# The scores and weighted sums of a pair of attention units, each spread over two neighbouring steps of the layer beside it

## The chip, the cores and the metric

The kernel runs on one core of a Trainium2 chip. The metric is the device time of one execution in microseconds (us), the median of several runs. The engines are named as in the profile: PE is TensorE's matmul, PEld its weight load, DVE is VectorE, ACT is ScalarE, POOL is GpSimd, SP is SyncE, whose queue (SPq) issues nearly all DMAs here.

## The reference, cut to what matters

Three stages follow one another: an attention with two kinds of masks, a gated layer, and a layer of eight experts with soft assignment to slots.

```
scores = q @ k.T / sqrt(64)          # 4 batches, 8 heads, 576 positions, head size 64
# heads 0-3: a window of 32 positions; heads 4-7: every 4th of 128 positions
attn = softmax(where(mask, scores, -1e9))
x = (attn @ v)                        # -> 2304 tokens x 512
y = (sigmoid(x @ w_gate) * (x @ w_val)) @ w_out        # 512 -> 1536 -> 512
logits = y @ phi                      # 32 slots
...                                   # soft dispatch, 8 experts, soft combination
```

## The kernel before, in words

**Blocks and units.** The 2304 tokens are worked on in five blocks, n = 0 to 4 (512 tokens each, the last 256). The attention of one block is cut into four units, one for each pair of heads (hp); 20 units in all. The masks leave only short windows, so a unit's scores are 32 small matmuls (`score`, L145: 64 rows by 32 columns of weights, 64 columns of data) and its weighted sums are 32 others (`weighted`, L208: 64 by 64; 16 for the plain heads of block 4). Each is shown twice in the profile, since the type is fp32: 64 matmuls and 64 weight loads for one unit's scores.

**The layer.** `l1` computes sigmoid and value of the gated layer for one block and one of 12 slices f of the 1536 columns. For each half a of a slice it runs 12 matmuls of 128x512 (L527) into one of two PSUM banks: for each of four chunks of x, high part of the weights with high and low part of x, then low part of the weights with the high part of x. ACT takes the first half's bank with a sigmoid (L537), DVE the second with a product (L539). Then it calls `between()`. One such group of 12 is a **step** here; blocks 0 and 1 have 24 steps each, counted 1 to 48. For a slice, `split_w` makes the high (ACT, L493) and low part (POOL and DVE, L494) of its weights; in block 0 from `convert` (DMA of the raw form, ACT, DVE, POOL, L421 to L442), in block 1 from a copy in DRAM that `load_w` reads back two slices at a time (L963, tile `wst`).

**The pairs.** Block 0's attention runs before the layer. The 16 units of blocks 1 to 4 run during steps 1 to 48, as eight pairs p = 0 to 7 (`Pairs`). `Pairs.__call__` is part of `between()`: at each step it runs what a table has due. For a pair these are
- `scores` at step SCORES_AT[p]: a mask matmul into each of two banks of `ps_a` (L140; four banks, shared with the turned tiles), 128 score matmuls, `softmax` (DVE max and subtraction, ACT exp, DVE sum and reciprocal, POOL product, L388), and the DMA of the next pair's q and k (L246);
- `turn` of each unit, TURN + TURN_LATE[p] steps later and one more: four transposes (L188) into a bank of `ps_a`, and an ACT copy (L189);
- `sums` at SUMS_AT[p]: the weighted sums into both banks of `ps_m`, the copies out (`finish`), and the DMA of v for the pair after the next (L253).

Block 4's units keep their scores inside the q/k buffer, so the q/k load of pair 7 can only start when the turns of pair 6 are done, unit by unit.

**What sets the order.** The functions are called in the order of the steps, but a scheduler places their instructions on each engine by its own estimate of readiness, within bounds: matmuls and transposes of the pairs (`kept`) stay in the order in which they are written, evictions of the layer's banks come ahead. Each engine, and SP's queue, then executes its list in order. Behind the first pairs two more things are mixed in: from step 25 on small transposes and matmuls of `slot_weights` (L468, L474, L483), and after block 0 the steps of `Post(0)` (L785 logits, L821 transposes, L831, L852, L878), which share the banks of `ps_a` and `ps_m`.

Of the kernel before, what the change touches and what calls it, by code (L numbers as in the profile page):

```python
# [7 lines left out]
F32 = mybir.dt.float32  # L8
# [9 lines left out]
P = 128  # L18
# [12 lines left out]
NRM = True  # L31
C0 = 21
SCORES_AT = (1, 8, 15, 22, 27, 32, 37, 41)
TURN = 4
TURN_LATE = (2, 0, 0, 0, 0, 0, 0, 1)
SUMS_AT = (10, 17, 25, 29, 34, 39, 44, 48)
C1 = 19
WP = 1
ND = 4
# [10 lines left out]
def k_window(n, hp, t, i):  # L50
    if n < 4:
        return 32 * (4 * t + i) if hp < 2 else 160 * i + 32 * t
    return 160 * t + 32 * i if hp < 2 else 64 * (4 * t + i)


def pb_tokens(n):
    return 512 if n < 4 else 256
# [3 lines left out]
def tile_kernel(  # L61
# [17 lines left out]
    ps_a = ctx.enter_context(tc.tile_pool(name="ps_a", bufs=4, space=PSUM))  # L79
    ps_m = ctx.enter_context(tc.tile_pool(name="ps_m", bufs=2, space=PSUM))  # L80
# [11 lines left out]
    mask = msk[:, 0:M_ID].rearrange("p (m c) -> p m c", m=3)  # L92
# [29 lines left out]
    kept = tc.keep_in_program_order  # L122
# [16 lines left out]
    def mask_at(bank, mask_):  # L139
        return nc.tensor.matmul(bank, lhsT=msk[:, M_ID:M_COLS], rhs=mask_, start=True, stop=False, skip_group_check=True)  # L140

    def score(u, t, i, r, to):
        n, hp = u["id"]
        o, d = k_window(n, hp, t, i), slice(64 * r, 64 * r + 64)
        return nc.tensor.matmul(  # L145
            to,
            lhsT=u["qk"][d, 128 * t + 32 * i : 128 * t + 32 * i + 32],
            rhs=u["qk"][d, 512 + o : 512 + o + 64],
            start=False,
            stop=True,  # L150
            skip_group_check=True,
        )

    def scores(u, ts):
        n, hp = u["id"]
        if "s_ps" not in u:
            u["s_ps"] = [ps_a.tile([P, 4, 64], F32, tag="a", name=f"s_ps{r}") for r in range(2)]
            for r in range(2):
                mask_at(u["s_ps"][r].rearrange("p t c -> p (t c)"), mask[:, 1 if hp >= 2 else 0])
        for t in ts:  # L160
            for i in range(4):
                for r in range(2):
                    score(u, t, i, r, u["s_ps"][r][32 * i : 32 * i + 32, t, :])
# [27 lines left out]
    def weighted(u, ts, xp, at=lambda x: x):  # L191

        n, hp = u["id"]
        dil = hp >= 2
        nq = 16 if n == 4 and dil else 32
        p_ = pt_ring[:, u["z"] % 4]
        v = u["v"].rearrange("p (t i r d) -> p t i r d", t=2, i=4, r=2)
        for t in ts:
            for i in range(2 if n == 4 and not dil else 4):
                for r in range(2):  # L200
                    for y in range(2):
                        o, k = xp[y][64 * r : 64 * r + 64, t], slice(64 * y, 64 * y + 64)
                        if dil:
                            o = o.rearrange("p (q f) -> p q f", f=4)[:, :, i]
                        else:
                            o = o[:, 32 * i : 32 * i + 32]
                        at(
                            nc.tensor.matmul(  # L208
                                o, lhsT=v[k, t, i, r, :], rhs=p_[k, 2 * r + t, i, 0:nq], start=True, stop=True
                            )  # L210
                        )
# [26 lines left out]
    def unit_loads(jobs, tags):  # L238
        us = [{"id": j, "z": z} for z, j in enumerate(jobs)]

        def load_qk(z):
            n, hp = jobs[z]
            w = 512 + k_cols(n, hp)
            us[z]["qk"] = b8(tags[z], [P, 2048], F32, "qk")
            us[z]["s"] = sm4[:, z % 4] if n < 4 else us[z]["qk"][:, 1536:2048]
            ld(nc.sync.dma_start(us[z]["qk"][:, 0:w], qkv[n * NHP + hp, :, VCOLS : VCOLS + w]))  # L246

        def load_v(z):
            n, hp = jobs[z]
            if z % 2 == 0:  # L250
                v2 = b8("v", [P, 2, VCOLS], F32, "v2")
                us[z]["v"], us[z + 1]["v"] = v2[:, 0], v2[:, 1]
            ld(nc.sync.dma_start(us[z]["v"], qkv[n * NHP + hp, :, 0:VCOLS]))  # L253

        return us, load_qk, load_v

    def first_attn(weights):
# [3 lines left out]
        def s_step(z, t):  # L261
            if z == 0 and t == 0:
                load_qk(0)
                ld(nc.sync.dma_start(msk, masks.bitcast(BF16)))
                load_qk(1)
                ld(nc.sync.dma_start(cst, consts))
                load_v(0)
                load_qk(2)
                load_v(1)
                weights()  # L270
                load_qk(3)
                load_v(2)
                load_v(3)
            scores(us[z], [t])
            if t == 3:
                softmax(us[z])
# [18 lines left out]
    class Pairs:  # L295


        def __init__(self):
            self.jobs = [(n, hp) for n in range(1, 5) for hp in HP_ORDER]
            self.us, self.qk, self.v = unit_loads(self.jobs, ["qk"] * 16)  # L300
            self.todo = []
            for p in range(8):
                t = SCORES_AT[p]
                late = t + TURN + TURN_LATE[p]
                self.todo += [(t, self.scores, p), (late, self.turn, 2 * p), (late + 1, self.turn, 2 * p + 1)]
                self.todo += [(SUMS_AT[p], self.sums, p)]
            self.todo.sort(key=lambda x: x[0])
            self.n = 0

        def __call__(self):  # L310
            self.n += 1
            while self.todo and self.todo[0][0] <= self.n:
                _, fn, p = self.todo.pop(0)
                fn(p)

        def load(self, what, p):
            if p < 8:
# [3 lines left out]
        def turn(self, z):  # L321
            turn_unit(self.us[z], ps_a, "a", kept)

        def scores(self, p):
            two = self.us[2 * p : 2 * p + 2]
            n = two[0]["id"][0]
            bank = [ps_a.tile([P, 512], F32, tag="a", name=f"s_ps{r}") for r in range(2)]
            for r in range(2):
                m_ = mask[:, 0:2] if n < 4 else mask[:, 2:3].to_broadcast([P, 2, 256])
                kept(mask_at(bank[r].rearrange("p (u c) -> p u c", u=2), m_))  # L330
            for y, u in enumerate(two):
                for t in range(4):
                    for i in range(4):
                        for r in range(2):
                            to = bank[r].rearrange("p (u t c) -> p u t c", u=2, t=4)
                            kept(score(u, t, i, r, to[32 * i : 32 * i + 32, y, t]))
            self.softmax(two, bank)
            self.load(self.qk, p + 1)
            if p == 0:
                self.load(self.v, 1)  # L340

        def sums(self, p):
            two = self.us[2 * p : 2 * p + 2]
            n, hp = two[0]["id"]
            xp = [ps_m.tile([P, 2, 2, pb_tokens(n) // 4], F32, tag="m", name=f"xp{y}") for y in range(2)]
            for y, u in enumerate(two):
                weighted(u, range(2), [x[:, y] for x in xp], kept)
            self.finish(n, hp % 2, xp)
            self.load(self.v, p + 2)

        def softmax(self, two, bank):
# [747 lines left out]
    for f in range(NF):  # L1099
        c = f % 4  # L1100
# [18 lines left out]
    for e in range(8):  # L1119
        for h in range(2):  # L1120
# [8 lines left out]
            tag = reuse.pop(0) if reuse else None  # L1129
# [11 lines left out]
        if e == 2:  # L1141
            rl = sc_[0:1, 192:320].rearrange("o (j s) -> o j s", j=4)
            sums = ps_m.tile([1, P], F32, tag="m", name="sums")
            nc.tensor.transpose(sums, lrun, ident)
            nc.vector.tensor_tensor(rl, re, sums.rearrange("o (j s) -> o j s", j=4), ALU.mult)
            rs = sc_[0:1, 320:352]
            nc.vector.tensor_reduce(rs, rl.rearrange("o j s -> o s j"), AX.X, ALU.add)
            nc.vector.tensor_scalar(rs, rs, 1e-9, None, ALU.add)
            nc.vector.reciprocal(rs, rs)
            nc.vector.tensor_copy(rl, rs.unsqueeze(1).to_broadcast([1, 4, 32]))  # L1150
            rcol = ps_m.tile([P, 1], F32, tag="m", name="rcol")
            nc.tensor.matmul(rcol, lhsT=rl.rearrange("o j s -> o (j s)"), rhs=ident[0:1, 0:1], start=True, stop=True)
            rc = sc_[:, 352:353]
            nc.vector.tensor_copy(rc, rcol)
# [201 lines left out]
```

## Time and profile before

| | |
|---|---|
| median of 3 runs | 499.6 us (498.39 to 499.72) |
| profiled execution, its own time | 498.51 us |
| its span, first to last instruction | 496.7 us |
| mean granted TensorE clock | 0.991 |
| busy, share of the span | PE 94%, PEld 72%, DVE 62%, ACT 49%, POOL 32% |

The span has five parts: a start-up with block 0's attention, steps 1 to 48 (about 35 to 232 us), a stage of blocks 2 and 3 together (to about 357 us), block 4's layer, and the experts. A busy PE includes the overlap of pipelined matmuls, so what counts in the steps is the distance from one group's first matmul to the next group's.

### The profile page before, as it was taken

The numbers are of one execution on the slowest core, as the hardware profiler recorded it, in microseconds if no ns is written. First come the engines' busy times: TensorE is split into PE (matmuls) and PEld (weight loads), VectorE is DVE, ScalarE is ACT, GpSimd is POOL, SyncE is SP. The second block draws the span as 40 slices with busy tenths as digits, with TensorE's granted clock in tenths as the row PEclk, the third lists the DMA queues.
The fourth block names the chain that finished last, engine by engine and source line by source line (L and its number), as shares of the span: only waits on it lengthen the run. The fifth ranks groups of instructions, "written<-read, shape, count | busy, mean of one in ns | idle before, by whom it ended". The sixth has DMA issues, their size and how long they took to land.

```text
span 496.7 us, 12722 instructions
## 1 busy us (share of the span) xinstructions
PE 467.2 (94%) x5470; PEld 356.4 (72%) x5476; DVE 306.4 (62%) x567; ACT 245.1 (49%) x422; POOL 159.7 (32%) x132
## 2 busy tenths in 40 slices
PE   6779999999899999999879999999999999999992
PEld 3558877878677877877448888888887889743552
DVE  3969698976767353554997656656548654531522
ACT  2467566746666453542954554554436544300232
POOL 0243555636283321182244342333312133110100
PEclk9899999999999999999999999999999999999997
DMA  8979899979976401750001220210599785589996
GB/s 325 407 258 345 278 368 313 340 253 376 406 271 212 172 3 49 259 189 3 0 11 76 84 78 9 84 48 38 199 379 422 296 357 215 204 303 379 423 382 217
DMA packets 23784, 112.13 MB, mean 226 GB/s; under 512 B 2352, under 2 KB 7216, under 8 KB 14640
## 3 DMA queue, kind: packets, MB, share of 16 engines
q1 hardware_dynamic: 23408, 111.06, 59.7%
q8 instruction: 43, 0.70, 0.5%
q10 hardware_dynamic: 320, 0.26, 0.2%
q14 instruction: 13, 0.11, 0.1%
HBM read 97.16 MB, written 14.16 MB: 224 GB/s over the span
## 4 chain that ended last, share of the span: by engine, by line
PE 72%; DVE 6%; DMA 4%; ACT 3%; issue 2%; POOL 1%; SPq 0%; DVEq 0%; ACTq 0%
PE l1ps L527 25%; PE pa L651 12%; PE pe L651 6%; PE tp L821 4%; PE h_ps L1122 3%; PE pd L651 3%; PE xp L208 3%; PE so_ps L1181 2%; DMA w<-wg 2%; PE sp L852 2%; PE lt_ps L785 2%; PE s_ps L145 2%; PE wt_ps L468 1%; DVE t_hl L554 1%; PE tr L188 1%
## 5 line engine op out<-in xcount | busy, mean ns | idle before, releaser
L527 PE MATMUL l1ps<-x_hi,whl 128*128 128x512 f32 x384 | 128.9, 402 | 3.2 <-ACT x_hi L229 2.5
L527 PEld LDWEIGHTS l1ps<-x_hi,whl 128*128 128x128 f32 x384 | 72.1, 189 | 20.1 <-ACT x_hi L229 3.2
L527 PE MATMUL l1ps<-x_lo,whl 128*128 128x512 f32 x192 | 76.1, 396 | 0.0
L442 POOL TENSOR_TENSOR fw<-fw 128x512 int32<-128x512 int32 x36 | 51.4, 1437 | 70.8 <-DVE fw L441 35.7
L539 DVE TENSOR_TENSOR g<-l1ps,g 128x512 f32<-128x512 f32 (+1 forms) x36 | 21.6, 600 | 33.6 <-PE l1ps L527 33.2
L527 PEld LDWEIGHTS l1ps<-x_lo,whl 128*128 128x128 f32 x192 | 36.5, 190 | 7.3 <-issue 0.4
L527 PE MATMUL l1ps<-x,whl 128*128 128x256 f32 x288 | 37.3, 286 | 0.1
L527 PEld LDWEIGHTS l1ps<-x,whl 128*128 128x128 f32 x288 | 35.4, 191 | 2.3 <-issue 1.7
L537 ACT ACTIVATE g<-l1ps 128x512 f32<-128x512 f32 (+1 forms) x36 | 18.9, 526 | 32.0 <-PE l1ps L527 31.9
L494 POOL TENSOR_TENSOR whl<-w,whl 128x512 fp32r<-128x512 f32 x12 | 15.9, 1327 | 52.3 <-ACT whl L493 40.7
L821 PE MATMUL tp<-cst,g 128*128 128x128 f32 x216 | 29.1, 275 | 0.1
L494 POOL TENSOR_TENSOR whl<-wst,whl 128x512 fp32r<-128x512 f32 x12 | 16.1, 1342 | 39.1 <-ACT whl L493 33.7
L439 ACT ACTIVATE fw<-st 128x512 f32<-128x512 f32 x36 | 22.7, 674 | 10.0 <-DMA st<-wd 10.0
L821 PEld LDWEIGHTS tp<-cst,g 128*128 128x128 f32 x216 | 24.1, 140 | 4.7 <-ACT g L537 1.7
L494 DVE TENSOR_TENSOR whl<-fw,whl 128x512 fp32r<-128x512 f32 x24 | 23.0, 963 | 6.7 <-ACT whl L493 6.1
L208 PEld LDWEIGHTS xp<-pt_ring,v 64*64 64x64 f32 x1216 | 19.2, 136 | 6.8 <-issue 3.8
L493 ACT CAST whl<-fw 128x512 fp32r<-128x512 f32 x24 | 14.7, 621 | 18.9 <-POOL fw L442 14.6
L826 ACT COPY gt<-tp 128x512 f32<-128x512 f32 x27 | 15.5, 581 | 16.0 <-PE tp L821 12.9
L441 DVE TENSOR_SCALAR fw<-st 128x512 int32<-128x512 uint32 x36 | 21.9, 635 | 2.4 <-DMA st<-wd 2.4
L720 DVE TENSOR_TENSOR tm<-pe,tm 128x512 f32<-128x512 f32 x12 | 8.3, 691 | 23.7 <-PE pe L651 23.7
L208 PE MATMUL xp<-pt_ring,v 64*64 64x32 f32 (+1 forms) x1216 | 20.7, 220 | 2.1 <-ACT pt_ring L189 1.6
L440 DVE TENSOR_SCALAR fw<-fw 128x512 uint32<-128x512 uint32 x36 | 21.0, 592 | 2.1 <-ACT fw L439 1.8
(464 smaller groups left out, 963.9 us busy)
## 6 DMA issues: line engine op xcount, KB each, us to landing
ew<-w SPq DMA_DIRECT2D x32, 1024.0 KB, 8.2
st<-wd SPq DMA_DIRECT2D x18, 1024.0 KB, 9.0
wst<-wg SPq DMA_DIRECT2D x12, 1024.0 KB, 6.8
v<-qkv SPq DMA_DIRECT2D x20, 512.0 KB, 6.5
wg<-fw SPq DMA_DIRECT2D x12, 512.0 KB, 8.0
w<-wg SPq DMA_DIRECT2D x6, 1024.0 KB, 7.6
qk<-qkv SPq DMA_DIRECT2D x10, 576.0 KB, 6.4
qk<-qkv SPq DMA_DIRECT2D x8, 528.0 KB, 5.8
```

Of the source, the lines that this page charges most:

```text
L208: nc.tensor.matmul(o, lhsT=v[k, t, i, r, :], rhs=p_[k, 2 * r + t, i, 0:nq], start=True, stop=True)
L439: nc.scalar.activation(top, st[:, c, 1].bitcast(F32), AF.Prelu, scale=2.0**-112, alpha=2.0**32)
L440: nc.vector.tensor_scalar(top.bitcast(U32), top.bitcast(U32), 3, None, ALU.logical_shift_left)
L441: nc.vector.tensor_scalar(low.bitcast(I32), st[:, c, 0], 2.0**-29, None, ALU.mult)
L442: nc.gpsimd.tensor_tensor(low.bitcast(I32), top.bitcast(I32), low.bitcast(I32), ALU.add)
L494: (nc.gpsimd if pool[h] else nc.vector).tensor_tensor(whl[:, 1, h], src[:, h], whl[:, 0, h].bitcast(F32), ALU.subtract)
L527: nc.tensor.matmul(pt[:, 0:nt], lhsT=whl[:, w_, a, dc, :], rhs=x_[n][:, dc, :], start=first, stop=(dc == HP_ORDER[-1] and w_ == 1),)
L537: nc.scalar.activation(g, pt[:, 0:nt], AF.Sigmoid)
L539: nc.vector.tensor_tensor(g, pt[:, 0:nt], g, ALU.mult)
L651: nc.tensor.matmul(pt, lhsT=w[:, w_, P * c : P * c + P], rhs=x_[:, c], start=first and c == 0 and w_ == 0 and x_ is hi, stop=c == 1 and w_ ...
L821: nc.tensor.transpose(tp[:, c], g_sb[self.n, 4 * q + c][:, P * j : P * j + P], ident)
L826: nc.scalar.copy(to, tp)
```

## The change

`scores` and `sums` are now called once for each unit of a pair, in two neighbouring steps (argument y). The first call takes the banks (and, for scores, writes the masks), the second ends with what followed before: softmax and the next q/k load, or the copies out and the next v load. The banks are kept between the calls in `self.at`. In the table, TURN goes from 4 to 5, counted from the first score step, with other TURN_LATE, so that pairs 1 to 6 turn one step later, and pairs 0 and 7 at the steps where they did. The first call for the sums of pairs 3 to 6 is one step later than the sums were, that of pair 7 one step earlier; pairs 0 to 2 start where they did.

```diff
-TURN = 4
-TURN_LATE = (2, 0, 0, 0, 0, 0, 0, 1)
-SUMS_AT = (10, 17, 25, 29, 34, 39, 44, 48)
+TURN = 5
+TURN_LATE = (1, 0, 0, 0, 0, 0, 0, 0)
+SUMS_AT = (10, 17, 25, 30, 35, 40, 45, 47)
...
-                self.todo += [(t, self.scores, p), (late, self.turn, 2 * p), (late + 1, self.turn, 2 * p + 1)]
-                self.todo += [(SUMS_AT[p], self.sums, p)]
+                self.todo += [(t + y, self.scores, p, y) for y in range(2)]
+                self.todo += [(late + y, self.turn, 2 * p + y) for y in range(2)]
+                self.todo += [(SUMS_AT[p] + y, self.sums, p, y) for y in range(2)]
...
-        def scores(self, p):
+        def scores(self, p, y):
             two = self.us[2 * p : 2 * p + 2]
             n = two[0]["id"][0]
...
+            if y == 0:
+                bank = self.at["s", p] = [ps_a.tile([P, 512], F32, tag="a", name=f"s_ps{r}") for r in range(2)]
+                for r in range(2):
+                    m_ = mask[:, 0:2] if n < 4 else mask[:, 2:3].to_broadcast([P, 2, 256])
+                    kept(mask_at(bank[r].rearrange("p (u c) -> p u c", u=2), m_))
+            bank = self.at["s", p]
+            for t in range(4):
+                for i in range(4):
+                    for r in range(2):
+                        to = bank[r].rearrange("p (u t c) -> p u t c", u=2, t=4)
+                        kept(score(two[y], t, i, r, to[32 * i : 32 * i + 32, y, t]))
+            if y == 0:
+                return
+            self.softmax(two, self.at.pop(("s", p)))
             self.load(self.qk, p + 1)
...
-        def sums(self, p):
+        def sums(self, p, y):
...
-            xp = [ps_m.tile([P, 2, 2, pb_tokens(n) // 4], F32, tag="m", name=f"xp{y}") for y in range(2)]
-            for y, u in enumerate(two):
-                weighted(u, range(2), [x[:, y] for x in xp], kept)
-            self.finish(n, hp % 2, xp)
+            if y == 0:
+                shape = [P, 2, 2, pb_tokens(n) // 4]
+                self.at["x", p] = [ps_m.tile(shape, F32, tag="m", name=f"xp{z}") for z in range(2)]
+            weighted(two[y], range(2), [x[:, y] for x in self.at["x", p]], kept)
+            if y == 0:
+                return
+            self.finish(n, hp % 2, self.at.pop(("x", p)))
             self.load(self.v, p + 2)
```

Two places on PE and one on SP's queue show what moves. The lines of the changed file are 8 higher from `finish` on (L527 is L535 there, L474 L482, L821 L829, L963 L971); a number behind a name tells tiles apart, and "..." stands for further matmuls of the same kind.

**PE, pair 4** (steps 27 and 28; qk_1603 and qk_1605 are its two units before, qk_1636 and qk_1638 after). Before, all scores stand in one run:

```order
L140 MATMUL s_ps1_1829<-msk_75 128x512
L145 MATMUL s_ps0_1828<-qk_1603 32x64
...
L145 MATMUL s_ps0_1828<-qk_1605 32x64
...
L474 MATMUL pt_ps_1912<-pm_91,cst_76 32x256 x4
L468 MATMUL wt_ps_1919<-cst_76,fw_1656 128x128 x4
L527 MATMUL l1ps_1925<-x_hi_1071,whl_1801 128x512
```

After:

```order
L140 MATMUL s_ps1_1823<-msk_75 128x512
L145 MATMUL s_ps0_1822<-qk_1636 32x64
...
L482 MATMUL pt_ps_1858<-pm_91,cst_76 32x256 x4
L476 MATMUL wt_ps_1865<-cst_76,fw_1656 128x128 x4
L535 MATMUL l1ps_1871<-x_hi_1102,whl_1795 128x512
...
L188 MATMUL tr_1885<-cst_76,sm4_172 128x128 x4
L145 MATMUL s_ps0_1822<-qk_1638 32x64
```

Between the two units now stand two kinds of small matmuls, 12 matmuls of the layer and a turn.

**PE, from the turn of pair 6's second unit to the layer's slice f = 10 of block 1** (qk_2242 and qk_2282 hold that unit; whl_3030 and whl_2975 are the split weights of slice 10, whl_2918 and whl_2912 those of slice 9). Before:

```order
L188 MATMUL tr_2900<-cst_76,qk_2242 128x128 x4
L821 MATMUL tp_2906<-cst_76,g_612 128x128 x4
L527 MATMUL l1ps_2923<-x_hi_1071,whl_2918 128x512
...
L145 MATMUL s_ps0_2727<-qk_2568 32x64
...
L527 MATMUL l1ps_2948<-x_hi_1071,whl_2918 128x512
...
L208 MATMUL xp0_2962<-pt_ring_90,v2_2380 64x32
...
L821 MATMUL tp_3024<-cst_76,g_976 128x128 x4
L527 MATMUL l1ps_3035<-x_hi_1071,whl_3030 128x512
```

After:

```order
L188 MATMUL tr_2931<-cst_76,qk_2282 128x128 x4
L829 MATMUL tp_2937<-cst_76,g_612 128x128 x4
L839 MATMUL dt_ps_2943<-cst_76,d_2810 128x128
L535 MATMUL l1ps_2948<-x_hi_1102,whl_2912 128x512
...
L829 MATMUL tp_2969<-cst_76,g_928 128x128 x4
L145 MATMUL s_ps0_2721<-qk_2589 32x64
...
L829 MATMUL tp_3018<-cst_76,g_928 128x128 x4
L535 MATMUL l1ps_2980<-x_hi_1102,whl_2975 128x512
```

Between the turn and slice 10 two groups of the layer and pair 6's weighted sums stood; now it is one group, and the sums come behind.

**SP's queue at the same place**, after (qk_2587 and qk_2589 are pair 7's units, wst_2600 the weights of slices 10 and 11):

```order
L246 DMA qk_2587<-qkv 128x1152
L246 DMA qk_2589<-qkv 128x1536
L971 DMA wst_2600<-wg32_5_86 128x2048
L253 DMA v2_2718<-qkv 128x1024 x2
L433 DMA wo32_2_89<-fw_2201 128x1024
```

These five stand in the same order before (`wst_2600` too): the load of slices 10 and 11 is issued behind the load of pair 7's second unit.

## Rows read from the trace of the kernel before

**Rows 1.** Windows: busy time and instructions of each engine, then clock and DMA
```profile
core 0: us, PE busy (x) PEld busy (x) DVE busy (x) ACT busy (x) POOL busy (x), PEclk, DMA share, GB/s
55.00:100.00 45.00, 43.85 (x680) 35.37 (x679) 39.41 (x66) 30.48 (x47) 24.52 (x18) 1.00 0.95 337
232.00:262.00 30.00, 25.07 (x204) 16.17 (x194) 27.53 (x53) 19.75 (x38) 8.97 (x7) 1.00 0.06 19
```

**Rows 2.** Waits of PE, 50 to 240 us: total, times, longest
```profile
PE s_ps L145 <- issue: 1.6, 1, 1.6
PE l1ps L527 <- ACT g L537: 0.8, 1, 0.8
PE s_ps L145 <- DMA qk<-qkv: 0.6, 1, 0.6
```

**Rows 3.** Timeline of PE, 81 to 92 us: start, length, instruction
```profile
81.88 1.48 PE L145 MATMUL s_ps<-qk 64*32 64x64 f32 x128
83.29 0.50 PE L527 MATMUL l1ps<-x_hi,whl 128*128 128x512 f32 x1
...
88.43 0.39 PE L527 MATMUL l1ps<-x_lo,whl 128*128 128x512 f32 x1
88.66 0.39 PE L527 MATMUL l1ps<-x_hi,whl 128*128 128x512 f32 x1
88.97 2.07 PE L208 MATMUL xp<-pt_ring,v 64*64 64x32 f32 x128
90.97 0.50 PE L527 MATMUL l1ps<-x_hi,whl 128*128 128x512 f32 x1
91.31 0.39 PE L527 MATMUL l1ps<-x_lo,whl 128*128 128x512 f32 x1
```

**Rows 4.** Timeline of PE at pair 4's scores; brackets: idle time before
```profile
125.88 1.38 PE L145 MATMUL s_ps<-qk 64*32 64x64 f32 x116
128.89 0.33 PE L145 MATMUL s_ps<-qk 64*32 64x64 f32 x12 [1.63 <-issue]
129.15 0.64 PE L474 MATMUL pt_ps<-pm,cst 128*32 128x256 f32 x8
```

**Rows 5.** DMA queues, whole span and 125.9 to 128.9: packets, MB, share
```profile
q8 instruction: 43, 0.70, 0.5%
...
q8 instruction: 1, 0.02, 2.3%
```

**Rows 6.** Timeline of PE and ACT at pair 1's first turn
```profile
71.12 0.66 PE L188 MATMUL tr<-cst,sm 128*128 128x128 f32 x4 [0.38 <-POOL sm L388]
...
70.61 1.28 ACT L537 ACT_TABLE_LOAD   x1
```

**Rows 7.** Timeline of PE, 195 to 212 us
```profile
195.57 0.86 PE L145 MATMUL s_ps<-qk 64*32 64x64 f32 x64 [0.62 <-DMA qk<-qkv]
196.35 0.42 PE L785 MATMUL lt_ps<-g,wp 128*32 128x128 f32 x6
...
200.12 0.60 PE L188 MATMUL tr<-cst,qk 128*128 128x128 f32 x4
200.55 0.60 PE L821 MATMUL tp<-cst,g 128*128 128x128 f32 x4
...
210.31 1.09 PE L821 MATMUL tp<-cst,g 128*128 128x128 f32 x8
211.16 0.47 PE L527 MATMUL l1ps<-x_hi,whl 128*128 128x512 f32 x1
```

**Rows 8.** Timeline of SP's queue there: issue of each DMA
```profile
200.86 0.33 SPq L246 DMA_DIRECT2D qk<-qkv  x1
201.24 0.43 SPq L963 DMA_DIRECT2D wst<-wg  x1
```

**Rows 9.** Timeline of ACT and POOL there: the split of slice 10
```profile
207.50 1.14 ACT L493 CAST whl<-wst 128x512 fp32r<-128x512 f32 x2 [1.80 <-DMA wst<-wg]
...
208.20 1.29 POOL L494 TENSOR_TENSOR whl<-wst,whl 128x512 fp32r<-128x512 f32 x1 [5.57 <-ACT whl L493]
```

More of the change, by code (lines that the diff above doesn't have):

```diff
@@ L304, in __init__ @@
                 late = t + TURN + TURN_LATE[p]
-                self.todo += [(t, self.scores, p), (late, self.turn, 2 * p), (late + 1, self.turn, 2 * p + 1)]
-                self.todo += [(SUMS_AT[p], self.sums, p)]
+                self.todo += [(t + y, self.scores, p, y) for y in range(2)]
+                self.todo += [(late + y, self.turn, 2 * p + y) for y in range(2)]
+                self.todo += [(SUMS_AT[p] + y, self.sums, p, y) for y in range(2)]
             self.todo.sort(key=lambda x: x[0])
+            self.at = {}
             self.n = 0
@@ L312, in __call__ @@
             while self.todo and self.todo[0][0] <= self.n:
-                _, fn, p = self.todo.pop(0)
-                fn(p)
+                _, fn, *args = self.todo.pop(0)
+                fn(*args)
         def load(self, what, p):
@@ L322, in turn @@
             turn_unit(self.us[z], ps_a, "a", kept)
-        def scores(self, p):
+        def scores(self, p, y):
             two = self.us[2 * p : 2 * p + 2]
             n = two[0]["id"][0]
[L327 to L330, printed above, removed]
-            for y, u in enumerate(two):
[L332 to L337, printed above, removed]
+            if y == 0:
[12 more added lines that the diff above has]
+            self.softmax(two, self.at.pop(("s", p)))
             self.load(self.qk, p + 1)
@@ L340, in scores @@
                 self.load(self.v, 1)
-        def sums(self, p):
+        def sums(self, p, y):
             two = self.us[2 * p : 2 * p + 2]
             n, hp = two[0]["id"]
-            xp = [ps_m.tile([P, 2, 2, pb_tokens(n) // 4], F32, tag="m", name=f"xp{y}") for y in range(2)]
-            for y, u in enumerate(two):
-                weighted(u, range(2), [x[:, y] for x in xp], kept)
-            self.finish(n, hp % 2, xp)
+            if y == 0:
[5 more added lines that the diff above has]
+            self.finish(n, hp % 2, self.at.pop(("x", p)))
             self.load(self.v, p + 2)
```

## The prediction

> **What bounds the kernel now.** I read the busy time by stretches first. From 55 to 100 us PE is busy 43.85 of 45.00 us, DVE 39.41; only after the steps, from 232 to 262, does PE fall behind, 25.07 of 30.00 against DVE's 27.53 [rows 1]. The reader is to see that through steps 1 to 48 PE is the engine without slack, at full clock. Then the waits of PE: between 50 and 240 us they come to four of note, 1.6 us on "issue", 0.8 on ACT, 0.6 on a DMA [rows 2] and 0.38 on POOL [rows 6]. So this change can gain at most some 4 us in the steps, by removing waits; whatever it adds to PE's own list is paid in full. The timeline of PE gives the price of each piece, taken from start to start. After the steps nothing is moved: the stage of blocks 2 and 3 starts with logits that need the last step, so what the steps lose or gain is passed on.
>
> **What the cuts cost on PE.** No matmul is added. What is added is places where PE passes from the layer's full-array matmuls to the small ones on parts of the array and back. Inside a group one follows the other after 0.23 us (88.43 to 88.66); the last before a run of weighted sums takes 0.31 (88.66 to 88.97), and the first behind it 0.34 (90.97 to 91.31) [rows 3]. So entering costs 0.08 to 0.09 and resuming 0.11. A run also has a fixed part of its own: 128 score matmuls take 1.41 us (81.88 to 83.29) [rows 3], 64 take 0.78 (195.57 to 196.35) [rows 7], which is 9.8 ns for each and 0.15 for the run. One more interruption of the layer is thus 0.35 us.
>
> How many there are I counted in the order of PE's instructions from pair 0's scores to the end of the steps: runs of weighted sums go from 8 to 16, runs of scores from 9 to 16 (pair 7's were apart before), and resumptions of the layer from 36 to 45; the other six new runs fall into places where other small work already interrupts it. The 15 runs cost 15 x 0.15 = 2.25 for their fixed parts. Of their entries 12 are from the layer (12 x 0.09 = 1.1), three from transposes, which the trace does not show for this pair; I take 0.1 each, near the others (0.3). Nine resumptions are 9 x 0.11 = 1.0. From this goes one: before, pair 7's scores cut the logits in two, after they do not, -0.35. **Sum: +4.3 us.** As bounds I keep 9 x 0.35 = 3.1 (only full interruptions count) and 4.7.
>
> [...]
>
> **What the cuts remove.** (1) Pair 4's scores stopped after 116 of 128 for 1.63 us with nothing to wait for but issue; the whole run took 125.88 to 129.15, 3.27 instead of 1.41 [rows 4]. In that stretch a packet of the instruction queue was under way; over the span there are 43 packets with 0.70 MB, 16 KB each [rows 5]. A unit pair's scores are 256 instructions (128 matmuls, 128 weight loads), issued in 1.41 us; PE ran out of them. Halved, 128 come, then a group of the layer with some 3 us for few instructions, then 128. The next packet is there by then. **-1.9.** The rest of the runs showed no such stop, so nothing more is gained there; if it only moves, nothing is gained at all. [...]
>
> (2) Pair 7's first scores waited 0.62 us for q and k, in the middle of the logits [rows 7]. Its load waits for the turn of pair 6's first unit; the turn is now a step later, and the scores come a group of the layer behind it and no longer inside the logits. **-0.6**, bound 0 if the load is still late.
>
> (3) At pair 1's first turn PE waited 0.38 us for POOL's product [rows 6] and then 0.8 for an eviction on ACT [rows 2], which stood behind other ACT work and a table load of 1.28 us from 70.61 [rows 6]. In the new order of ACT that table load and the eviction come ahead of the copies of pair 0's sums. The softmax starts a step later and is needed a step later, so the first wait I leave. **-0.8**, bounds 0 and -1.2.
>
> **What the moved turn makes late.** Turning one step later is hidden for pairs 1 to 5: the sums follow later too. Not for pair 6. SP issues pair 7's second q/k load only after that unit's turn (PE at 200.12, issue at 200.86), and the weights of slices 10 and 11 stand right behind it in the queue, at 201.24 [rows 7, 8]. They landed when ACT's first cast could start, 207.50; POOL made the low part from 208.20 to 209.49 [rows 9]; the group began at 211.16 [rows 7]. So the low part is ready 9.4 us after the turn starts (209.49 - 200.12), the high part of the first half about 8.0 (half of ACT's two casts). Before, PE took 11.04 us from the turn to the group, so it never waited. After, between them stand: the turn 0.43, one Post transpose group 0.43 [rows 7], a small one (about 0.2, like half of those), one group of the layer 0.23 x 12 + 0.11 = 2.87 [rows 3], eight transposes 0.85, scores 0.78 and eight transposes 0.85 [rows 7] plus 0.1 for an entry: 6.5 us. The group would start at 6.5 and need the low part 0.8 later (0.34, 0.23, and 0.23 for a matmul of the other half that stands between), at 7.3; it gets it at 9.4. **+2.0 us.** Bounds: 0, if the weights land 2 us sooner, and 3, if the load is as slow and pair 7's softmax, queued on ACT behind the cast that waits, then holds the next turn. Behind the waiting group stand pair 6's sums and pair 7's turns, so all of it is passed on.
>
> The banks: the sums now hold both `ps_m` banks over a step more, with `slot_weights` behind them; ACT and DVE have room to copy them out by the time PE asks again, 0.8 us later. I put this at 0, up to 1 if ACT is behind.
>
> **Sum.** +4.3 - 1.9 - 0.6 - 0.8 + 2.0 = +3.0 us. On the profiled execution's own time, 498.5, that is 501.5. The median of the runs is 499.6, 1.1 above it; the upper end of the range allows for that.
>
> **Rivals.**
> - *The weights' wait doesn't come.* It decides at 2 us: had the load of slices 10 and 11 taken 4.3 us from issue instead of 6.3 (207.50 - 201.24), the group would not wait. It shares the DMA with the q/k load ahead and v behind it, as before, which speaks for 6.3. Without it: +1.0, 499.5, not slower by what can be measured.
> - *It is worse.* The stop of 1.9 us moves to another run, or the wait for weights grows into pair 7's turn: +4 to +5, 503. Speaks for it: DVE is busy 39.41 of 45 us early on [rows 1], so a softmax that starts a step later has little room; against: each pair keeps its distance from second scores to turn.
> - *It is faster.* The whole price of the cuts rests on passages; if a half beside other small work costs no more than its matmuls, only the full interruptions are left, 3.1, and if the weights come in time as well, and all of pair 1's wait goes, it is 3.1 - 1.9 - 0.6 - 1.2 = -0.6; a clear gain would need further waits to go that this execution doesn't show (other runs stood at 499.7). About 497.
> - *It doesn't do what it says*: pair 0's two calls are only two layer matmuls apart in the new order, pair 7's were apart already. The other six are separated, so this is no more than a quarter of the effect.
>
> **How the numbers follow.** What can be told from no change is 0.3%, 1.5 us. The forecast has 0.50 (its own range 500 to 503), the missing wait 0.25, the worse case 0.13, the faster one 0.12. Of the forecast's 0.50, a fifth falls within 1.5 us, of the missing wait's nearly all, so: slower 0.55, same 0.30, faster 0.15. The range leaves out the faster case and the end of the worse one: 498.6 to 504.0.
>
> **What would show it.** Right: no idle time on "issue" at pair 4's scores; score and sum runs of 64 at about 0.8 and 1.0 us with 0.31 ahead and 0.34 behind; no DMA wait in the logits; ACT's cast of slice 10 waiting for `wst`, PE idle before the low part's matmul of that slice. Wrong: issue waits in halves, no idle time at slice 10, or PE waits of over 1 us that I don't name, above all at the turns of pairs 1 to 3.

## The result, and the profile after

The changed kernel takes 506.18 us (median of 6 runs, 503.98 to 508.39), the one before 499.35 (6 runs beside it): ratio 1.0128, 95% interval 1.0094 to 1.0162. It is slower, by 6.8 us; I had said 501.5. The profiled execution of it took 506.9 us, span 505.0, mean granted clock 0.982 (before 498.51, 496.7, 0.991).

The waits of PE between 50 and 240 us, in us in total, times, longest (answers to [rows 2]):

```profile
PE l1ps L535 <- ACT whl L501: 1.6, 1, 1.6
PE s_ps L145 <- DMA qk<-qkv: 1.3, 1, 1.3
PE l1ps L535 <- ACT g L545: 0.7, 1, 0.7
PE l1ps L535 <- POOL whl L502: 0.3, 1, 0.3
PE wp_ps L491 <- DVE pt L486: 0.3, 1, 0.3
```

The stop on issue is gone, and the wait in the logits. In their place stand three waits within some 6 us, at slice 10. The timeline of PE there (start, length, instruction, idle time before it; answers to [rows 7]):

```profile
205.41 0.66 PE L188 MATMUL tr<-cst,qk 128*128 128x128 f32 x4
...
209.23 1.03 PE L829 MATMUL tp<-cst,g 128*128 128x128 f32 x8
211.60 0.86 PE L145 MATMUL s_ps<-qk 64*32 64x64 f32 x64 [1.33 <-DMA qk<-qkv]
212.39 1.09 PE L829 MATMUL tp<-cst,g 128*128 128x128 f32 x8
215.07 0.50 PE L535 MATMUL l1ps<-x_hi,whl 128*128 128x512 f32 x1 [1.59 <-ACT whl L501]
215.41 0.40 PE L535 MATMUL l1ps<-x_lo,whl 128*128 128x512 f32 x1
215.65 0.45 PE L535 MATMUL l1ps<-x_hi,whl 128*128 128x512 f32 x1
216.44 0.95 PE L535 MATMUL l1ps<-x_hi,whl 128*128 128x512 f32 x2 [0.34 <-POOL whl L502]
217.19 0.63 PE L535 MATMUL l1ps<-x_lo,whl 128*128 128x512 f32 x1
217.62 1.05 PE L535 MATMUL l1ps<-x_hi,whl 128*128 128x512 f32 x2
...
220.51 0.67 PE L208 MATMUL xp<-pt_ring,v 64*64 64x32 f32 x32
```

The reader is to see two things. PE stands first for pair 7's q and k, then for the split weights of slice 10. And from 216.44 on the layer's matmuls are 0.43 us apart (217.19 to 217.62), not 0.23. The windows say why (us, busy time and instructions of each engine, granted clock, DMA share, GB/s): the granted clock fell from 1.00 to 0.50 behind the waits, and once more behind the wait of 1.96 us in the stage of blocks 2 and 3.

```profile
214.00:216.00 2.00, 0.93 (x3) 0.48 (x3) 1.51 (x5) 1.68 (x4) 0.90 (x1) 1.00 0.86 285
216.00:218.00 2.00, 1.66 (x5) 1.28 (x5) 2.00 (x3) 1.99 (x4) 0.38 (x1) 0.69 1.04 426
218.00:220.00 2.00, 2.00 (x6) 1.57 (x5) 1.93 (x4) 1.80 (x3) 1.35 (x2) 0.50 0.92 383
220.00:222.00 2.00, 2.00 (x38) 1.40 (x38) 0.48 (x2) 1.10 (x2) 2.00 (x2) 0.95 0.08 33
...
268.00:270.00 2.00, 2.00 (x6) 1.58 (x5) 2.00 (x2) 0.33 (x1) 1.23 (x1) 0.50 1.00 393
```

The timeline of SP's queue and of ACT there (answers to [rows 8, 9]):

```profile
206.21 0.33 SPq L246 DMA_DIRECT2D qk<-qkv  x1
206.59 0.94 SPq L971 DMA_DIRECT2D wst<-wg  x1
...
214.40 1.14 ACT L501 CAST whl<-wst 128x512 fp32r<-128x512 f32 x2 [0.30 <-DMA wst<-wg]
```

The weights took 7.8 us from issue to the cast (214.40 - 206.59), 6.3 before.

**Where the 6.8 us are.** In each trace I took PE's time from pair 0's mask matmul (L140, at 35.23 us before and 35.91 after) to the first matmul of the stage of blocks 2 and 3 (238.95 and 246.43), and took from it the idle time that the timeline tags. The rest is PE's own list, at whatever clock. In us:

| kernel | this stretch | tagged waits | rest | clock below 0.99 |
|---|---|---|---|---|
| before | 203.72 | 3.65 | 200.07 | nowhere |
| changed | 210.52 | 4.17 | 206.35 | 216 to 222 |
| experiment 1 (pair 6 turned earlier) | 206.02 | 1.63 | 204.39 | nowhere |
| experiment 2 (weights first) | 208.89 | 2.82 | 206.07 | 212 to 218 |
| experiment 3 (before, pair 6 turned later) | 204.77 | 4.10 | 200.67 | nowhere |
| experiment 4 (moved, not cut) | 206.97 | 5.13 | 201.84 | 96 to 102 |
| experiment 10 (late turn, earlier sums, weights first) | 206.30 | 1.84 | 204.46 | nowhere |

The stretch grew by 6.80 us, as the medians did. The span grew by 8.3: 0.7 of it lie before the stretch and 0.8 behind it. Half clock stands in both places (in the changed kernel at 12 to 16, 24 to 30 and 268 to 272 us, before at 20 to 24), and other executions have or lack it there (below); that it alone makes these 1.5 us isn't shown.

### The profile page after: what moved, and what is told of

It is laid out like the page before. It is cut to its first block, busy times and chain, and to the rows that moved or that the text cites. A ratio compares the mean times of both kernels' runs of the same rounds, so it can differ in the third digit from the quotient of the medians.

```text
span 505.0 us, 12723 instructions
## 1 busy us (share of the span) xinstructions
PE 475.5 (94%) x5469; PEld 359.4 (71%) x5476; DVE 307.3 (61%) x567; ACT 245.4 (49%) x422; POOL 157.8 (31%) x132
## 4 chain that ended last, share of the span: by engine, by line
PE 85%; DVE 5%; ACT 3%; DMA 3%; issue 1%; SPq 1%; DVEq 0%; ACTq 0%
PE l1ps L535 34%; PE pa L659 12%; PE pe L659 6%; PE tp L829 4%; PE xp L208 4%; PE so_ps L1189 3%; PE pd L659 3%; PE h_ps L1130 3%; PE lt_ps L793 3%; PE s_ps L145 3%; PE sp L860 2%; PE tr L188 2%; DMA v<-qkv 1%; DMA qk<-qkv 1%; PE wt_ps L476 1%
## 5 line engine op out<-in xcount | busy, mean ns | idle before, releaser
L535 PE MATMUL l1ps<-x_hi,whl 128*128 128x512 f32 x384 | 132.5, 408 | 4.6 <-ACT x_hi L229 2.0
L535 PEld LDWEIGHTS l1ps<-x_hi,whl 128*128 128x128 f32 x384 | 72.7, 190 | 22.2 <-ACT x_hi L229 2.7
L535 PE MATMUL l1ps<-x_lo,whl 128*128 128x512 f32 x192 | 77.1, 401 | 0.0
L450 POOL TENSOR_TENSOR fw<-fw 128x512 int32<-128x512 int32 x36 | 50.0, 1396 | 74.3 <-DVE fw L449 35.0
L535 PEld LDWEIGHTS l1ps<-x_lo,whl 128*128 128x128 f32 x192 | 36.9, 192 | 7.1 <-issue 0.4
L535 PE MATMUL l1ps<-x,whl 128*128 128x256 f32 x288 | 37.2, 286 | 0.0
L535 PEld LDWEIGHTS l1ps<-x,whl 128*128 128x128 f32 x288 | 35.4, 191 | 2.1 <-issue 1.9
L829 PE MATMUL tp<-cst,g 128*128 128x128 f32 x216 | 29.3, 276 | 0.1
L829 PEld LDWEIGHTS tp<-cst,g 128*128 128x128 f32 x216 | 24.1, 140 | 5.5 <-ACT g L545 1.7
L208 PE MATMUL xp<-pt_ring,v 64*64 64x32 f32 (+1 forms) x1216 | 22.3, 220 | 1.9 <-issue 1.2
L502 DVE TENSOR_TENSOR whl<-fw,whl 128x512 fp32r<-128x512 f32 x24 | 21.5, 914 | 3.3 <-ACT whl L501 2.8
L449 DVE TENSOR_SCALAR fw<-st 128x512 int32<-128x512 uint32 x36 | 20.5, 595 | 3.6 <-DMA st<-wd 3.6
```

Source lines behind the costliest of these rows:

```text
L208: nc.tensor.matmul(o, lhsT=v[k, t, i, r, :], rhs=p_[k, 2 * r + t, i, 0:nq], start=True, stop=True)
L449: nc.vector.tensor_scalar(low.bitcast(I32), st[:, c, 0], 2.0**-29, None, ALU.mult)
L450: nc.gpsimd.tensor_tensor(low.bitcast(I32), top.bitcast(I32), low.bitcast(I32), ALU.add)
L502: (nc.gpsimd if pool[h] else nc.vector).tensor_tensor(whl[:, 1, h], src[:, h], whl[:, 0, h].bitcast(F32), ALU.subtract)
L535: nc.tensor.matmul(pt[:, 0:nt], lhsT=whl[:, w_, a, dc, :], rhs=x_[n][:, dc, :], start=first, stop=(dc == HP_ORDER[-1] and w_ == 1),)
L829: nc.tensor.transpose(tp[:, c], g_sb[self.n, 4 * q + c][:, P * j : P * j + P], ident)
```

## The experiments

Each was timed beside the kernel before (499.5 to 499.9 us there). I give the median, the ratio to before and its 95% interval.

**1. The turns of pair 6 back to where they were**, all cuts kept.

```diff
-TURN_LATE = (1, 0, 0, 0, 0, 0, 0, 0)
+TURN_LATE = (1, 0, 0, 0, 0, 0, -1, 0)
```

> The changed kernel with one number of its table different: pair 6's turns stand one step earlier (steps 41 and 42, as before the change), all cuts stay. Theory A (what the change loses is lost at slice 10 of block 1: the weights stand in SP's queue behind pair 7's q/k load, which waits for the turn of pair 6's second unit; PE then waits 1.33 us for q and k, 1.59 and 0.34 for the split weights, and runs some 2.2 us longer at half clock): 506.2 - 5.5 = about 500.7, with no wait at slice 10. Theory B (the cuts themselves cost it, and slice 10 is only where the time shows): 505 or more.

Measured: 502.47 us, 1.0054 (1.0030 to 1.0077). All waits of PE from 50 to 240 us:

```profile
PE s_ps L145 <- DMA qk<-qkv: 0.7, 1, 0.7
PE l1ps L535 <- ACT g L545: 0.7, 1, 0.7
PE wp_ps L491 <- DVE pt L486: 0.3, 1, 0.3
```

The waits at slice 10 are gone and the clock stays, as theory A says. But 2.6 us remain, more than the 1 us or so that I allowed, so there is a price besides these waits. The table sizes it: rest 204.39 - 200.07 = 4.3 us. That it belongs to the cuts and not to what was moved, experiment 4 shows.

**2. The weights ahead of pair 7's q/k load in SP's queue**, turns late (the next stage's first load is held behind; on PE eight transposes moved from ahead of slice 10 to behind its first group).

```diff
+            self.todo.append((39, self.load, self.qk, 7))
...
-            self.load(self.qk, p + 1)
+            if p != 6:
+                self.load(self.qk, p + 1)
```

> The changed kernel with the load of slices 10 and 11 issued ahead of pair 7's q/k load in SP's queue; the turns of pair 6 stay late and PE's order stays nearly the same. Theory A: the two waits at slice 10 (1.9 us) and the half clock behind them (2.2 us) go, the wait of pair 7's second scores for q and k (1.33 us) stays or shrinks: 506.2 - 4.1 = about 502. Theory B: 505 or more. If not the place in the queue but the shared DMA is what makes the load late, nothing changes in the sum, since q and k then come later: 505 to 506.

Measured: 503.99 us, 1.0093 (1.0056 to 1.0130). The wait for the weights is gone, the one for q and k grew from 1.33 to 1.94, since that load now took 6.0 us, and the clock fell behind it:

```profile
210.00:212.00 2.00, 0.15 (x2) 0.00 (x0) 1.90 (x3) 1.01 (x3) 1.91 (x2) 1.00 0.94 185
212.00:214.00 2.00, 1.91 (x67) 1.63 (x68) 1.03 (x2) 0.00 (x0) 2.00 (x2) 0.71 0.89 340
214.00:216.00 2.00, 2.00 (x6) 1.54 (x5) 1.58 (x5) 0.68 (x1) 2.00 (x3) 0.50 1.06 434
```

So the place in the queue makes the weights late. The time lies between theory A (about 502) and its rivals (505 and more): the stretch is 1.6 us shorter than in the changed kernel, and the two medians' intervals overlap. In this execution a single wait of 1.94 us was followed by half clock.

**3. Before, with pair 6's turns a step later.**

```diff
-TURN_LATE = (2, 0, 0, 0, 0, 0, 0, 1)
+TURN_LATE = (2, 0, 0, 0, 0, 0, 1, 1)
```

> The kernel before with one number of its table different: pair 6's turns one step later (steps 42 and 43), nothing cut. Theory A: slice 10 waits here too: 499.4 + 3 to 5.5 = 502.4 to 505, with the wait for the split weights in the trace. Theory B: 499.4, within 1.5 us.

Measured: 500.56 us, 1.0017 (0.9984 to 1.0051). Theory A missed. PE at slice 10:

```profile
206.61 0.88 PE L208 MATMUL xp<-pt_ring,v 64*64 64x32 f32 x46
207.82 0.86 PE L145 MATMUL s_ps<-qk 64*32 64x64 f32 x64 [0.33 <-DMA qk<-qkv]
208.61 0.98 PE L208 MATMUL xp<-pt_ring,v 64*64 64x16 f32 x50
...
212.40 0.73 PE L527 MATMUL l1ps<-x_hi,whl 128*128 128x512 f32 x2 [0.52 <-POOL whl L494]
```

Pair 6's sums, whole and at step 44, stand here between the turn and slice 10 and cover the loads. In this execution the late turn costs 1.0 us of waits there and keeps the clock; for the loss it takes the later sums as well. The trace is of the fastest of the 12 runs (498.47 us); the slowest took 506.74, and what those waited for isn't shown.

**4. Moved, not cut**: both units in the step of the second.

```diff
-                self.todo += [(t + y, self.scores, p, y) for y in range(2)]
+                self.todo += [(t + 1, self.scores, p, y) for y in range(2)]
...
-                self.todo += [(SUMS_AT[p] + y, self.sums, p, y) for y in range(2)]
+                self.todo += [(SUMS_AT[p] + 1, self.sums, p, y) for y in range(2)]
```

> The changed kernel with nothing cut: both units' scores stand in the step in which the second stood, both units' sums too; softmax, turns, copies out and loads stay in their steps. Theory A with the prediction's prices (cuts +4.3, pair 4's stop for instructions comes back, +1.9): 506.2 - 4.3 + 1.9 = 503.8, the waits at slice 10 stay. Theory B: 499 to 500.

Measured: 503.28 us, 1.0066 (1.0039 to 1.0092), near the 503.8 of theory A, but by another sum. Slice 10 waits 0.9 us here; a stop on issue of 3.2 us came, not at pair 4's scores but at pair 1's sums, with half clock behind it:

```profile
91.61 2.06 PE L208 MATMUL xp<-pt_ring,v 64*64 64x32 f32 x126
96.89 0.24 PE L208 MATMUL xp<-pt_ring,v 64*64 64x32 f32 x2 [3.21 <-issue]
97.06 0.71 PE L535 MATMUL l1ps<-x_hi,whl 128*128 128x512 f32 x1
```

This run is the control for the price of the cuts. Its rest is 201.84; the matmuls behind the stop, at half clock, took 1.6 us longer than at full clock (eight distances in 3.50 us, from 97.06 to 100.56, not in 0.34 + 7 x 0.23). Without that it is 200.3, an estimate, 0.2 above before. So the moves cost PE nearly nothing, and the 4.3 us of experiment 1 belong to the cuts.

**5 and 6. Experiment 1 with one half of the cuts each**: scores cut, sums joined (5), and the reverse (6), by the edits of experiment 4.

> Pair 6's turns early as in the first experiment, scores cut, sums joined in the step of their second half. Theory A (every cut has its price on PE, and a long run can outrun the instruction refill): the sums' share of the price goes, 8 runs at 0.13 us and some four resumptions of the layer at 0.26, about 2.1 us, so 502.5 - 2.1 = 500.4; if a stop for instructions appears in a run of 128 sums, 2 to 3 us more. Theory C (the price of the first experiment is not from the cuts but from the moved turns): 502 to 503.

> Pair 6's turns early, sums cut, scores joined in the step of their second half. Theory A: the scores' share goes, 7 runs at 0.10 us and some four resumptions at 0.26, about 1.7 us, but a stop for instructions in a run of 128 scores can come back, 1.3 to 1.9: 502.5 - 1.7 = 500.8, or about 502.5 with the stop, which the trace then shows as idle time on issue. Theory C: 502 to 503 without a stop.

Measured: 502.38 us, 1.0062 (1.0038 to 1.0085), and 504.10 us, 1.0082 (1.0051 to 1.0113). Both stopped on issue at pair 1's sums, 1.95 and 3.22 us, with half clock behind. In experiment 6 these sums were halved:

```profile
92.31 1.13 PE L208 MATMUL xp<-pt_ring,v 64*64 64x32 f32 x62
96.66 0.32 PE L208 MATMUL xp<-pt_ring,v 64*64 64x32 f32 x2 [3.22 <-issue]
```

So a run of half the length stops too: a half is not safe in itself, as the prediction had taken it to be. What the place in the stream has to do with it, experiments 7, 13 and 14 ask. The time of experiment 5 fits theory A with a stop and theory C alike; that of experiment 6 lies above both, by a stop and half clock longer than I had allowed. The rests tell the theories apart: 203.80 and 205.04, less 1.4 and 2.2 for the half clock (worked out as in experiment 4, from 97.05 to 100.14 and from 96.91 to 101.77), are 202.4 and 202.8, estimates. Against 200.3 with no cut, the scores' cuts alone cost some 2.1 us and the sums' some 2.5, which speaks for theory A.

**7. Before, with pair 4's scores alone cut**, the first unit a step earlier.

```diff
-                self.todo += [(t, self.scores, p), (late, self.turn, 2 * p), (late + 1, self.turn, 2 * p + 1)]
+                self.todo += [(t - (p == 4) * (1 - y), self.scores, p, y) for y in range(2)]
+                self.todo += [(late, self.turn, 2 * p), (late + 1, self.turn, 2 * p + 1)]
```

> The kernel before with the scores of pair 4 alone cut, the first unit one step earlier; all else stays. Theory A with the prediction's prices: the stop of 1.63 us goes (1.9 with its cut resumption), one interruption of 0.35 comes: 499.9 - 1.5 = 498.4. Rival: the stop moves to another run, since what lies ahead of it in the instruction stream is as long as before: 499.9 or a little more, with idle time on issue elsewhere.

Measured: 500.12 us, 0.9996 (0.9967 to 1.0025). The stop stayed, at the same matmul (after 52 of the second 64, so 116 of 128, as in [rows 4]), with 0.92 us. What the cut moved stood ahead of that matmul before and after, so the same number of PE's instructions (4030 in both traces) is in front of it:

```profile
126.72 0.76 PE L145 MATMUL s_ps<-qk 64*32 64x64 f32 x52
128.39 0.33 PE L145 MATMUL s_ps<-qk 64*32 64x64 f32 x12 [0.92 <-issue]
```

**8. The changed kernel with PE kept busy ahead of slice 10.**

```diff
+            if (n, f, a) == (1, 10, 0):
+                for _ in range(6):
+                    kept(
+                        nc.tensor.matmul(
+                            pt,
+                            lhsT=msk[:, M_ID:M_COLS],
+                            rhs=msk[:, 0:512],
+                            start=True,
+                            stop=True,
+                            skip_group_check=True,
+                        )
+                    )
```

> The changed kernel with six extra 128x512 matmuls (their result is overwritten) ahead of the first matmul of slice 10 in block 1, where PE otherwise waits 1.59 us for the split weights. They fit into the wait (6 x 0.23 = 1.4). If the waits bring the half clock, and keeping PE busy in the last of them keeps the clock: 506.2 - 2.2 = 504.0, with full clock from 214 to 222 us. If the wait for q and k of 1.33 us ahead of them brings it already, or the clock has another cause: 506, or up to 1 us more where the extra matmuls come late.

Measured: 506.44 us, 1.0133 (1.0101 to 1.0166), runs at 504.7 to 505.3 and at 507.6, three each. In the profiled one, of 504.73, the clock stayed:

```profile
212.00:216.00 4.00, 3.68 (x80) 2.62 (x81) 2.82 (x7) 1.36 (x3) 0.68 (x1) 1.00 0.98 352
216.00:220.00 4.00, 3.66 (x45) 2.62 (x44) 3.44 (x6) 3.97 (x5) 0.86 (x2) 1.00 0.97 406
```

From the first matmul of step 44 to the sums behind slice 10's first group it took 13.0 us (206.11 to 219.14), not 14.1 (206.37 to 220.51), although the wait for q and k was 2.12 us this time. But then a later matmul waited 0.59 for DVE, and the median is no lower. That the half clock costs is shown in the trace; that filling the wait pays is not.

**9. The changed kernel with pair 6's sums at steps 44 and 45.**

```diff
-SUMS_AT = (10, 17, 25, 30, 35, 40, 45, 47)
+SUMS_AT = (10, 17, 25, 30, 35, 40, 44, 47)
```

> The changed kernel with pair 6's weighted sums one step earlier (steps 44 and 45), its turns stay late. Their first half (0.8 us with its passages) then stands ahead of pair 7's second scores and of slice 10, and covers part of the waits there. Theory A (the price is that too little work stands between the late turn and what its loads release): the wait for q and k falls from 1.33 to about 0.5, the one for the split weights from 1.93 to 1 to 1.9, and with them the half clock may stay away: 506.2 less 1 to 3 = 503 to 505. If the sums only move and PE waits as long for the loads: 505.5 to 506.5.

Measured: 507.26 us, 1.0159 (1.0120 to 1.0198). Missed: q and k were still waited for, 1.19 us, transposes 0.68 for ACT's copies, the split weights 0.63, and the clock fell from 216 to 222. With the q/k load at 5.3 us, one run of sums is too little cover.

**10. Experiments 2 and 9 together** (the table also names a later step for pair 7's second scores; PE's order there is that of experiment 9).

> The changed kernel with pair 6's turns still late, but its sums one step earlier and the weights of slices 10 and 11 ahead of pair 7's q/k load in SP's queue. Theory A: no wait for the weights, about 0.5 to 1.3 us for q and k, and less half clock: the first experiment's time plus that wait, 502.5 + 0 to 1.5 = 502.5 to 504. Theory B (what is lost lies elsewhere): 505 or more.

Measured: 503.35 us, 1.0092 (1.0059 to 1.0124), within theory A. The second q/k load took 4.2 us here and nothing waited for it (the first cost 0.2); the rest is 204.46, that of experiment 1. So with a late turn too the price of the place goes away, if nothing waits. How much of that is the weights' place in the queue and how much the shorter q/k load (5.3 us in experiment 9) isn't told apart.

**11 and 12. Two versions that might beat both.** Six filling matmuls where PE waits in the stage of blocks 2 and 3, in the kernel before (11); the same with the edit of experiment 7 (12).

```diff
+        if f == 1:
+            for _ in range(6):
+                kp(
+                    nc.tensor.matmul(
+                        pd, lhsT=msk[:, M_ID:M_COLS], rhs=msk[:, 0:512], start=True, stop=True, skip_group_check=True
+                    )
+                )
         if prev:
             product(pa, pw["a22"], "t4", False)
```

> The kernel before with six extra 128x512 matmuls (their result is overwritten) where PE waits 1.96 us for DVE in the stage of blocks 2 and 3; nothing else differs. They take 6 x 0.23 = 1.4 us and fit into the wait. If a wait of PE of some 2 us brings four us of half clock in a part of the executions, and that makes the scatter of the times: full clock at this place in the profiled execution, fewer times above 501, the median 0 to 1 us lower, 498.8 to 499.8. If the clock doesn't hang on such waits: the median and the scatter stay, or the median rises by what the matmuls push.

> The kernel before with both edits that cost nothing in their traces: pair 4's scores alone cut, and the six extra matmuls in the wait of the stage of blocks 2 and 3. If the shorter stop for instructions at pair 4's scores (0.92 instead of 1.63 us, the steps 1.3 us shorter in that trace) is a gain of each execution, and the clock is kept after the wait: 499.5 - 1.3 = 498.2, a ratio of about 0.997. Rival (the stop's length varies between executions as much as that, so the steps gained nothing): 499.2 to 499.8, no difference.

Measured: 499.16 us, 0.9995 (0.9975 to 1.0015), and 498.99 us, 0.9987 (0.9968 to 1.0007). In both the clock stayed at 1.00 behind this wait (0.66 us of it were left in each). Neither is shown to be faster than the kernel before.

**13 and 14. PE's instruction stream shifted**, by 64 and 32 more tiny matmuls at the start of the kernel before.

```diff
-SMALL = 70
+SMALL = 134
```

> The kernel before with 64 more of the tiny matmuls with which PE starts (32 columns, no result is used): 128 instructions more in PE's stream ahead of everything, half a packet of the 43 that carry PE's 10,946 matmuls and weight loads. If the place of a stop is where a packet ends in the stream: no stop after the 116th of pair 4's 128 scores, stops of up to 3 us at other runs or none; the time 499.5 less 1.6 or plus up to 3. If a run of 256 instructions outruns the refill wherever it stands, as the prediction had it: pair 4's scores stop as before, 1 to 1.6 us; time 499.5 to 500.2 (the tiny matmuls take 0.7 us at the start, partly beside the first loads).

> The same with 32 more tiny matmuls, 64 instructions, a quarter of a packet. If the end of a packet decides: the stop in pair 4's scores moves by 32 matmuls towards the start of the run, to about the 84th of 128, or goes. If the run's length decides: it stays at the 116th, 1 to 1.6 us.

Measured: 506.10 us, 1.0132 (1.0112 to 1.0152), and 500.70 us, 1.0020 (0.9999 to 1.0041). Pair 4's 128 scores run without a stop in both. The timeline of PE in experiment 13, first these scores, then the long stops that it has elsewhere, two of them in block 0's attention:

```profile
131.17 1.48 PE L145 MATMUL s_ps<-qk 64*32 64x64 f32 x128
...
11.85 1.06 PE L145 MATMUL s_ps<-qk 64*32 64x64 f32 x51 [4.00 <-issue]
...
24.28 0.42 PE L145 MATMUL s_ps<-qk 64*32 64x64 f32 x4 [3.28 <-issue]
...
217.46 0.60 PE L821 MATMUL tp<-cst,g 128*128 128x128 f32 x4 [1.81 <-issue]
```

The place in the stream makes a stop possible, not the length of the run, and the traces show which place. In all 16 of them PE stops on issue 41 times for over 0.35 us. Counted in order of start over PE's matmuls, its weight loads and the few waits of its sequencer that the trace records, each stop stands behind the 190th to 194th of a group of 256, and each ends 1.2 to 1.6 us after a packet of the instruction queue (q8 in [rows 5]) has landed. So in these traces a stop of that length is PE waiting for its next packet, at a place that comes every 256 instructions; the 43 packets of [rows 5] to the 10,946 matmuls and weight loads of that trace are 255 each.

Whether PE stops there hangs on when the packet comes. At pair 1's sums the same place was reached in both: in experiment 6 PE ran out at 93.44 us, the packet landed at 95.33, PE went on at 96.66. In experiment 1 the packet had landed at 93.81, and these sums ran through:

```profile
94.21 1.14 PE L208 MATMUL xp<-pt_ring,v 64*64 64x32 f32 x64
95.28 0.50 PE L535 MATMUL l1ps<-x_hi,whl 128*128 128x512 f32 x1
```

A packet that comes late makes a long stop (1.89 us late and 3.22 us of stop in experiment 6). What sets when it comes stays open.

## Why the prediction was wrong

The direction was right, by the mechanism named, and the size was not: +3.0 us predicted, +6.8 measured, outside the range. By its own terms:

| term | predicted | measured | from |
|---|---|---|---|
| cuts on PE | +4.3 | +4.3 | rest of experiment 1 less before, 204.39 - 200.07 |
| pair 4's stop | -1.9 | -1.9 | 1.63, and a stop of 0.25 at pair 0 (36.88 us) that the term didn't have; both gone |
| pair 7's q and k | -0.6 | +0.7 | 0.62 in the logits gone, as put; 1.33 new, at the second half |
| pair 1's waits | -0.8 | -0.5 | ACT 0.77 to 0.65, POOL's 0.38 gone |
| weights of slice 10 | +2.0 | +1.9 | 1.59 and 0.34 |
| a new wait for `pt` | 0 | +0.3 | 0.26 |
| half clock | not in the sum | +2.0 | rest, 206.35 - 204.39 |
| sum | +3.0 | +6.8 | |

Two steps failed, and they make 3.3 of the missing 3.8 us.

**The first is the one on pair 7's q and k.** I priced the wait of the first scores alone, and let the second scores stand in the sum of 6.5 us without one. But the second of the two loads was at its limit before, which I had not looked up. The timeline of PE in the kernel before:

```profile
205.06 0.86 PE L145 MATMUL s_ps<-qk 64*32 64x64 f32 x64
```

and its DMA issues there (size, us from issue to landing):

```profile
qk<-qkv SPq DMA_DIRECT2D x1, 768.0 KB, 4.1
```

Issued at 200.86 [rows 8], it landed at 204.96, 0.1 us ahead of its scores. The prediction's own terms left no slack either: from the turn to these scores 0.43 + 0.43 + 0.2 + 2.87 + 0.85 + 0.1 = 4.9 us, from the turn to the landing 0.74 + 4.1 = 4.8. After, PE was ready for them at 210.27 (211.60 - 1.33), 4.1 us behind the issue at 206.21, and this time the load took longer (DMA issues of the changed kernel):

```profile
qk<-qkv SPq DMA_DIRECT2D x1, 768.0 KB, 5.3
```

So this wait is one of those "of over 1 us that I don't name". The order of the changed kernel took only 0.1 us from the load's time; 1.2 are the slower load. Why it took 5.3 to 6.1 us in the changed kernel and in experiments 2, 8 and 9, and 4.0 to 4.3 in the others (experiment 12's trace has no time for it), three of them with a late turn (3, 4, 10), stays open.

**The second, and the larger, is the clock.** The sum priced waits at their own length and had no term for it. Behind 3.3 us of them within some 6 the thirteen matmuls of slice 10 up to the next sums took 5.10 us (215.07 to 220.51 without the 0.34). In experiment 1 twelve stand there and take 2.94:

```profile
212.37 0.47 PE L535 MATMUL l1ps<-x_hi,whl 128*128 128x512 f32 x1
...
215.31 0.67 PE L208 MATMUL xp<-pt_ring,v 64*64 64x32 f32 x32
```

With one more at 0.23 that is 3.17, so the half clock cost 1.9 here, near the 2.0 of the table. Experiments 1 and 10, without such waits, lack it.

**Point by point.** The price of the cuts held to a tenth of a us. So did the wait for weights, but by luck: the load itself was 1.5 us slower than I took it, and PE, 1.33 us late for q and k, met it that much later. Experiment 2 confirms the queue as its cause, experiment 3 corrects the reason: it takes the sums behind slice 10 as well as the late turn.

The stop at pair 4's scores went, and here for the reason given. The place of 256 still lies in pair 4's scores, now behind some 25 of the second unit's 64. Before, PE ran out at 127.26 us and the packet landed at 127.48. In the changed kernel it landed at 128.24, a group of the layer now stood between the two units, and the second ran through, 4.2 us behind the landing:

```profile
132.46 0.86 PE L145 MATMUL s_ps<-qk 64*32 64x64 f32 x64
```

What was wrong is that a half is safe by its length: experiment 6 stops in one, and experiment 7, whose cut brought the first unit forward and left PE as early at the place (127.47 us, the packet landed at 127.11), stops too.

Of pair 1's waits ACT's eviction, on which the term of -0.8 stood, hardly moved; the 0.38 that went is POOL's, which I had left standing. The banks cost next to nothing, as put. Of the rivals, "worse" is nearest: it had the wait for weights grow into pair 7's turn; it was pair 7's scores, and the clock, that took the rest.

## What to carry to other kernels

Price a wait at its length and at what it may do to the clock: here a wait of 1.9 us was followed by half clock in eight executions and not in six, and the half clock behind waits and stops of 1.95 to 3.3 us cost 1.4 to 2.2 us more (estimates of experiments 4 to 6, and the 1.9 of the changed kernel). Before a step is moved, measure the slack of every transfer that its release starts, also of those that show no wait now; in a list of waits 0.1 us of slack looks like plenty. And a stop on instruction supply belonged here to a place in the stream, every 256 instructions, and to a packet that came late: 128 and 64 instructions more ahead moved the place (experiments 13 and 14, no stop in pair 4's scores), so the going of a stop is not a gain to count on.

## What the runs showed of the hardware

**The same wait drops the clock or doesn't.** PE's wait for DVE in the stage of blocks 2 and 3 was 1.91 to 1.96 us in all 14 profiled executions that didn't fill it with matmuls. In eight of them (changed, 1, 4, 7, 9, 10, 13, 14) the clock then fell to 0.50, for 3.4 us in the changed kernel (windows: 0.50 at 268 to 270, 0.65 at 270 to 272), in six (before, 2, 3, 5, 6, 8) it stayed; with filling matmuls (11, 12) it stayed both times. After the fall, the six matmuls behind the wait took 2.44 us in the changed kernel (267.62 to 270.06), against 1.51 before. What decides between a fall and none isn't shown.

**The scatter of one kernel goes in part with the clock.** The six executions of the changed kernel had spans of 502.1, 502.9, 503.6, 504.9, 505.0 and 506.5 us at mean clocks of 0.992, 0.985, 0.989, 0.986, 0.982 and 0.982.

**64 tiny matmuls at the start cost 6 us** (experiment 13), though they compute nothing that is used. In its trace stops of 4.00 and 3.28 us stand in block 0's attention (before, one of 1.61 us, at 11.82), and pair 0's mask matmul stands at 40.02 us and not at 35.23. Half as many (experiment 14) moved it to 40.19 in the trace, but the median of its 12 runs is no higher than noise allows; the traced one, of 504.13 us, is among its slowest.
